# One 128-channel GpSimd add for a batch's logits instead of two 64-channel ones, and a new table of places

## The chip, the cores and the metric

The kernel runs on one core of a Trainium2 chip. The time is the device time of one execution in microseconds (us), and less is better. Engines are named as the profile names them: PE (TensorE matmuls; PEld its weight loads), DVE (VectorE), ACT (ScalarE), POOL (GpSimd), SP (the queue that issues most DMAs).

## The reference, cut to what matters

Two layers stand behind one another. The first is attention with a hash mask, for 4 batches of 8 heads, 768 positions and 64 columns a head; the second is a soft mixture of 8 experts with 4 slots each, over the 3,072 rows of 512 columns that the first one gives.

```python
mask = q_bucket[:, :, :, None] == k_bucket[:, :, None, :]      # 6 sign bits of q @ proj, k @ proj
scores = np.where(mask, scale * q @ k.T, -1e9)
attn = softmax(scores); x = (attn @ v) as (batch*position, head*column)
logits = x @ phi                                  # 3072 x 32
d = softmax of logits over the 3072 rows;  slot_input = d.T @ x
slot_out[e] = relu(slot_input[e] @ w1[e]) @ w2[e] # 8 experts
out = softmax of logits over the 32 slots @ slot_out
```

## The kernel before, in words

The 32 heads run through one software pipeline. Of a head, `smax` (L692) multiplies the keys with the queries once for the row maxima, and `most` (L701, L704) takes these on DVE out of two PSUM buffers, so PE can be at most two such products ahead of DVE. `shift` and `shift_rows` (L730 to L744) turn the maxima into a row of the operand: DVE, one PE transpose, an ACT copy, and a DMA on the SP queue (L744, told under the helper's line L600, as `XY<-mr`). `scores` (L755) multiplies a second time with the shift included, `exps` (L761) takes the exponential on ACT, `av` (L782) multiplies with v, and `acc` (L769, L772) adds the exponentials' tiles on POOL for the denominator, one 128x768 add at a time.

Heads go in pairs. Ahead of each pair `split_hi` (L592, ACT) and `split_lo` (L596) cut q and k in two parts; `split_lo` is one 128x768 subtraction on DVE and one on POOL, both with two operands in SBUF. After a pair, `pair_sum`, `pair_turn`, `pair_rec`, `pair_log`, `pair_add` and `pair_x` (L789 to L843) normalise it, write x and add its share of the logits to a tile `lacc` (128x384). The two halves of `lacc`'s 128 channels hold two partial sums, of even and odd heads.

After four pairs a batch is complete. `batch_both` (L885) adds the two halves and puts the sum on both: ACT copies channels 64 to 127 of `lacc` to channels 0 to 63 of `dl` (L889), then POOL adds twice on 64 channels (L891), first into the upper half of `dl`, then in place into the lower one. `batch_max` (L902 to L910) takes the maxima on DVE, and `batch_exp`, `batch_turn`, `batch_slots` and the like carry the batch into the slots. That happens inside the pipeline for batches 0 to 2; the last batch is done at the end by `one_sum` to `one_fold`, without `batch_both`.

The order of the work is written by hand and no tool moves it: three tables, `WHEN` (a place for each step of a pair), `FIRST` and `LAST` (for the first and the last heads), give each step a place counted in slots of a sixth of a head; `at` (L1043) puts the steps in a list, the list is sorted by place, and the steps are issued in that order. Each engine and the SP queue then run their own instructions strictly in this order. Weights of the experts are loaded between the heads (`load_weights`, 512 KB a piece). After the last head come the expert multiplications (L1198, L1251) and the output (L1274).

Of the kernel before, what the change touches and what calls it, by code (L numbers as in the profile page):

```python
# [76 lines left out]

FIRST = {('bits', 0): -102.0988,
 ('first_x', 0): -24.247,
 ('first_x', 1): -39.392,  # L80
 ('first_x', 2): -29.078,
 ('first_x', 3): -19.8151,
 ('load', 4, 0): -5.2093,
 ('load', 4, 1): -3.4609,
 ('bits', 2): -21.6367,
 ('split_hi', 2): -5.8363,
 ('split_lo', 2, 0): 0.2624,
 ('split_lo', 2, 1): -4.3782,
 ('spread_y', 2): -4.8648,
 ('spread_bits', 2): -12.8087,  # L90
 ('spread_l', 2): 6.144,
 ('spread_x', 2): 3.6219,
 ('smax', 1, 0, 0): -22.4884,
 ('smax', 1, 0, 1): -14.425,
 ('smax', 1, 1, 0): -13.675,
 ('smax', 1, 1, 1): -18.5454,
 ('smax', 1, 2, 0): -15.9696,
 ('smax', 1, 2, 1): -10.3836,
 ('smax', 1, 3, 0): -10.2744,
 ('smax', 1, 3, 1): -13.2403,  # L100
 ('smax', 1, 4, 0): -12.705,
 ('smax', 1, 4, 1): -11.4718,
 ('smax', 1, 5, 0): -8.4134,
 ('smax', 1, 5, 1): -17.6068,
 ('first_y', 1): -98.0409,
 ('first_y', 2): -23.6654,
 ('spread_y', 1): -34.1549,
 ('spread_l', 0): -19.5111,
 ('spread_bits', 1): -31.1275,
 ('bits_rest',): -39.0243,  # L110
 ('bits_copy', 0): -61.5875,
 ('bits_copy', 1): -49.0932,
 ('first_w', 0, 0): -52.9271,
 ('first_w', 0, 1): -45.0627,
 ('copy_ident',): -30.4055,
 ('bits_out',): -17.6073,
 ('shift_first', 0): -28.1207,
 ('rows_first', 0): -22.8276,
 ('shift_first', 1): -21.3284,
 ('rows_first', 1): -19.3923,  # L120
 ('most', 1, 0): -21.0299,
 ('most', 1, 2): -12.6994,
 ('most', 1, 3): -17.9276,
 ('most', 1, 4): -14.489,
 ('most', 1, 6): -5.6202,
 ('most', 1, 7): -10.9525,
 ('most', 1, 8): -7.0455,
 ('most', 1, 10): -4.4109,
 ('most', 1, 11): -16.3298,
 ('bits_first', 1): -52.2068,  # L130
 ('split_hi', 0): -104.3439,
 ('split_lo', 0, 0): -33.2942,
 ('split_lo', 0, 1): -24.2451,
 ('spread_x', 0): -18.4484,
 ('load_v', 0): -49.1631,
 ('smax', 0, 0, 0): -57.7206,
 ('scores', 0, 0, 0): -18.4489,
 ('most', 0, 0): -31.1109,
 ('exps', 0, 0): -16.2704,
 ('smax', 0, 0, 1): -54.4021,  # L140
 ('scores', 0, 0, 1): -17.5476,
 ('smax', 0, 1, 0): -48.1338,
 ('scores', 0, 1, 0): -16.9955,
 ('most', 0, 2): -29.8189,
 ('exps', 0, 2): -12.7003,
 ('smax', 0, 1, 1): -89.3202,
 ('scores', 0, 1, 1): -7.715,
 ('most', 0, 3): -45.7527,
 ('exps', 0, 3): -4.37,
 ('smax', 0, 2, 0): -81.0645,  # L150
 ('scores', 0, 2, 0): -13.5826,
 ('most', 0, 4): -32.0633,
 ('exps', 0, 4): -8.1301,
 ('smax', 0, 2, 1): -44.5826,
 ('scores', 0, 2, 1): -9.075,
 ('smax', 0, 3, 0): -38.6124,
 ('scores', 0, 3, 0): -5.9648,
 ('most', 0, 6): -29.6441,
 ('exps', 0, 6): -4.235,
 ('smax', 0, 3, 1): -38.4796,  # L160
 ('scores', 0, 3, 1): -14.8362,
 ('most', 0, 7): -28.5666,
 ('exps', 0, 7): -9.8986,
 ('smax', 0, 4, 0): -28.5933,
 ('scores', 0, 4, 0): -17.6084,
 ('most', 0, 8): -28.1478,
 ('exps', 0, 8): -12.8511,
 ('smax', 0, 4, 1): -25.4573,
 ('scores', 0, 4, 1): -13.1315,
 ('smax', 0, 5, 0): -23.7083,  # L170
 ('scores', 0, 5, 0): -1.5997,
 ('most', 0, 10): -22.8582,
 ('exps', 0, 10): 2.4486,
 ('smax', 0, 5, 1): -26.4348,
 ('scores', 0, 5, 1): -2.4708,
 ('most', 0, 11): -24.7664,
 ('exps', 0, 11): 2.5416,
 ('av', 0, 0): -11.6598,
 ('acc', 0, 1): 2.9017,
 ('av', 0, 1): -1.251,  # L180
 ('acc', 0, 2): 3.8826,
 ('av', 0, 2): -0.8419,
 ('acc', 0, 3): 4.5951,
 ('av', 0, 3): -0.6937,
 ('acc', 0, 4): 4.8395,
 ('av', 0, 4): 4.2016,
 ('acc', 0, 5): 11.46,
 ('av', 0, 5): 9.6883,
 ('spread_l', 1): -28.2578,
 ('spread_x', 1): -17.2822,  # L190
 ('load_v', 1): -33.0257,
 ('scores', 1, 0, 0): 1.3496,
 ('exps', 1, 0): 3.8687,
 ('scores', 1, 0, 1): 4.6498,
 ('scores', 1, 1, 0): 7.2362,
 ('exps', 1, 2): 8.0704,
 ('scores', 1, 1, 1): 4.1294,
 ('exps', 1, 3): 5.5945,
 ('scores', 1, 2, 0): 0.8493,
 ('exps', 1, 4): 3.2616,  # L200
 ('scores', 1, 2, 1): 1.752,
 ('scores', 1, 3, 0): 3.2247,
 ('exps', 1, 6): 5.1221,
 ('scores', 1, 3, 1): 10.8661,
 ('exps', 1, 7): 12.8423,
 ('scores', 1, 4, 0): 2.9321,
 ('exps', 1, 8): 10.0997,
 ('scores', 1, 4, 1): 6.0124,
 ('scores', 1, 5, 0): 9.855,
 ('exps', 1, 10): 11.8275,  # L210
 ('scores', 1, 5, 1): 10.5008,
 ('exps', 1, 11): 13.3899,
 ('shift', 1): -3.8039,
 ('shift_rows', 1): -2.6775,
 ('av', 1, 0): 11.9568,
 ('acc', 1, 1): 8.8476,
 ('av', 1, 1): 12.6368,
 ('acc', 1, 2): 11.415,
 ('av', 1, 2): 12.6451,
 ('acc', 1, 3): 14.0042,  # L220
 ('av', 1, 3): 12.9619,
 ('acc', 1, 4): 18.9427,
 ('av', 1, 4): 13.579,
 ('acc', 1, 5): 21.4429,
 ('av', 1, 5): 16.4939,
 ('load', 2, 0): -49.4921,
 ('load', 2, 1): -52.2068,
 ('load_v', 2): 10.2435,
 ('smax', 2, 0, 0): -4.103,
 ('scores', 2, 0, 0): 16.667,  # L230
 ('most', 2, 0): -2.8532,
 ('exps', 2, 0): 16.9649,
 ('smax', 2, 0, 1): 5.9825,
 ('scores', 2, 0, 1): 13.8757,
 ('smax', 2, 1, 0): 6.6523,
 ('scores', 2, 1, 0): 15.6577,
 ('most', 2, 2): 8.8854,
 ('exps', 2, 2): 16.8927,
 ('smax', 2, 1, 1): -0.3316,
 ('scores', 2, 1, 1): 13.8393,  # L240
 ('most', 2, 3): 2.2782,
 ('exps', 2, 3): 14.9992,
 ('smax', 2, 2, 0): 2.8055,
 ('scores', 2, 2, 0): 13.5895,
 ('most', 2, 4): 6.6529,
 ('exps', 2, 4): 16.0579,
 ('smax', 2, 2, 1): -1.9582,
 ('scores', 2, 2, 1): 17.72,
 ('smax', 2, 3, 0): 1.2515,
 ('scores', 2, 3, 0): 19.3082,  # L250
 ('most', 2, 6): 3.5218,
 ('exps', 2, 6): 19.3709,
 ('smax', 2, 3, 1): -3.7661,
 ('scores', 2, 3, 1): 16.8244,
 ('most', 2, 7): 0.5334,
 ('exps', 2, 7): 17.2995,
 ('smax', 2, 4, 0): 4.0474,
 ('scores', 2, 4, 0): 17.7324,
 ('most', 2, 8): 8.0087,
 ('exps', 2, 8): 19.7556,  # L260
 ('smax', 2, 4, 1): 5.8646,
 ('scores', 2, 4, 1): 19.2004,
 ('smax', 2, 5, 0): 8.5568,
 ('scores', 2, 5, 0): 20.167,
 ('most', 2, 10): 9.3556,
 ('exps', 2, 10): 20.2925,
 ('smax', 2, 5, 1): 4.1508,
 ('scores', 2, 5, 1): 17.3078,
 ('most', 2, 11): 8.6656,
# [1073 lines left out]
```

## Time and profile before

| | |
|---|---|
| median of 3 runs | 485.52 us (481.4, 485.52, 1116.75) |
| profiled execution | 484.55 us, its span 482.8 us |
| mean granted TensorE clock | 0.972 |
| PE busy | 452.3 us (94%), 3975 matmuls |
| DVE busy | 361.5 us (75%) |
| ACT busy | 276.9 us (57%) |
| POOL busy | 356.2 us (74%) |
| chain that ended last | PE 85%, DVE 6%, DMA 4%, ACT 2% |

The span is the time from the first to the last instruction of the profiled execution. A share of busy time is a mean over the whole span; the chain is the sequence of instructions and waits that ended last, followed back from the end.

### The profile page before, as it was taken

To read this page: it belongs to the slowest core of one execution; us is meant where nothing else is said; L and a number is where in the kernel's file an instruction comes from. 1 tells how busy PE (TensorE), PEld (TensorE's weight loads), DVE (VectorE), ACT (ScalarE), POOL (GpSimd) and SP (SyncE) were. 2 spreads that over 40 slices of the span, in tenths; PEclk is the share of its full clock that TensorE was granted. 3 is DMA by queue.
4 is the path that set the end of the run, shared out by engine and by line. 5 is a ranking of instruction groups with operands and counts; after the bars stand their busy time and mean duration, and the time that the engine had idled before them with its cause. 6 is when DMAs were issued, how large, how long until landed. Compare 5 with 4: busy or idle time off the path is not lost.

```text
span 482.8 us, 10644 instructions
## 1 busy us (share of the span) xinstructions
PE 452.3 (94%) x3975; PEld 280.5 (58%) x3975; DVE 361.5 (75%) x669; ACT 276.9 (57%) x568; POOL 356.2 (74%) x223
## 2 busy tenths in 40 slices
...
GB/s 190 123 190 159 136 150 152 164 160 210 153 92 205 135 216 150 226 139 228 136 142 143 202 157 169 201 170 176 98 183 128 67 167 331 342 380 331 412 302 304
DMA packets 37703, 93.18 MB, mean 193 GB/s; under 512 B 7106, under 2 KB 13380, under 8 KB 37652
## 3 DMA queue, kind: packets, MB, share of 16 engines
...
q8 instruction: 31, 0.51, 0.4%
q10 hardware_dynamic: 240, 0.34, 0.2%
...
## 4 chain that ended last, share of the span: by engine, by line
PE 85%; DVE 6%; DMA 4%; ACT 2%; issue 1%; SPq 0%; DVEq 0%; ACTq 0%
PE st L755 28%; PE av L782 23%; PE smx L692 15%; DVE w L596 4%; PE qs L1251 3%; PE qh L1198 3%; PE mi L639 3%; PE mi L794 2%; PE mi L819 2%; DMA w<-w 1%; PE mi L740 1%; PE av L548 1%; DMA XY<-mr 1%; PE mi L957 1%; ACT w L592 1%
## 5 line engine op out<-in xcount | busy, mean ns | idle before, releaser
L772 POOL TENSOR_TENSOR acc<-acc,pt 128x768 f32<-128x768 f32 x125 | 232.7, 1865 | 11.9 <-ACT pt L761 6.7
L761 ACT ACTIVATE pt<-st 128x512 f32<-128x512 f32 x288 | 163.5, 594 | 89.0 <-PE st L755 87.2
L755 PE MATMUL st<-XY 128*128 128x256 f32 (+1 forms) x768 | 181.4, 348 | 2.1 <-DMA XY<-mr 1.2
L704 DVE TENSOR_REDUCE mx<-smx 128x1 f32<-128x512 f32 x192 | 131.6, 688 | 49.0 <-PE smx L692 46.3
L755 PEld LDWEIGHTS st<-XY 128*128 128x128 f32 x768 | 127.7, 194 | 23.6 <-issue 4.5
L692 PE MATMUL smx<-XY 96*128 96x256 f32 (+1 forms) x384 | 123.2, 362 | 15.6 <-DVE mx L704 14.8
L782 PE MATMUL av<-pt,v 128*32 128x384 f32 x1536 | 137.7, 489 | 0.0
L692 PEld LDWEIGHTS smx<-XY 96*128 96x128 f32 x384 | 71.4, 194 | 49.0 <-DVE mx L704 18.8
L782 PEld LDWEIGHTS av<-pt,v 128*32 128x32 f32 x1536 | 45.4, 109 | 67.7 <-issue 55.0
L769 POOL TENSOR_TENSOR acc<-pt 128x768 f32<-128x768 f32 x32 | 58.6, 1832 | 32.9 <-ACT pt L761 32.9
L701 DVE TENSOR_REDUCE mx<-smx 128x2 f32<-128x512 f32 x96 | 65.6, 685 | 4.7 <-PE smx L692 3.8
L596 DVE TENSOR_TENSOR w<-raw,w 128x768 fp32r<-128x768 f32 x14 | 37.5, 2677 | 1.9 <-issue 0.5
L596 POOL TENSOR_TENSOR w<-raw,w 128x768 fp32r<-128x768 f32 x16 | 35.1, 2196 | 0.0
L797 ACT ACTIVATE sm<-mi,eps 128x384 f32<-128x384 f32 x15 | 8.7, 579 | 30.4 <-PE mi L794 30.4
L592 ACT CAST w<-raw 128x768 fp32r<-128x768 f32 x30 | 23.6, 831 | 0.5 <-DMA XY<-w 0.2
L609 ACT CAST XY<-w 64x768 fp32r<-64x768 f32 x30 | 23.3, 825 | 0.0
L786 ACT COPY avs<-av 128x384 f32<-128x384 f32 x32 | 15.2, 476 | 12.2 <-PE av L782 12.0
L842 DVE TENSOR_TENSOR xq<-mi,r 128x384 f32<-128x384 f32 x30 | 16.7, 558 | 2.2
L841 DVE STREAM_TRANSPOSE mi<-avs 128x384 f32<-128x384 f32 x30 | 17.4, 582 | 0.8 <-ACT mr L743 0.7
L811 ACT COPY r<-rt 64x12 f32<-64x12 f32 x60 | 11.9, 199 | 7.1 <-DVE rt L803 6.4
L1251 PE MATMUL qs<-w 128*32 128x128 f32 (+1 forms) x360 | 14.9, 304 | 0.0
L801 DVE STREAM_TRANSPOSE sm<-sm 128x384 f32<-128x384 f32 x15 | 8.7, 578 | 7.4 <-ACT sm L797 7.2
...
## 6 DMA issues: line engine op xcount, KB each, us to landing
...
```

The costliest lines, as they stand in the source:

```text
L592: nc.scalar.copy(st[h]["w4"][:, 2 * x], st[h]["raw", x])
L596: (nc.vector if h > 2 and x == 0 else nc.gpsimd).tensor_tensor(out=w[:, 2 * x + 1], in0=st[h]["raw", x], in1=w[:, 2 * x], op=ALU.subtract)
L609: nc.scalar.copy(s["Y"][0:64, x], s["w4"][0:64, 2 * x])
L692: nc.tensor.matmul(pt[:, o:o + b - a], s["Y"][0:96, 0, t * P:(t + 1) * P], s["Y"][0:96, 1, a:b], start=True, stop=True)
L701: nc.vector.tensor_reduce(out=mx[:, n - 1:n + 1], in_=s["sm_ps", n - 1].rearrange("p (a x) -> p a x", a=2), axis=AX.X, op=ALU.max)
L704: nc.vector.reduce_max(out=mx[:, n:n + 1], in_=s["sm_ps", n], axis=AX.X)
L755: nc.tensor.matmul(pt[:, o:o + b - a], x[:, 1, i * P:(i + 1) * P], x[:, 0, a:b], start=first, stop=not first)
L761: nc.scalar.activation(s["P", n // 4][:, 512 * u:512 * u + 512], s["st_ps", n - (n % 4 == 2)], AF.Exp, scale=D ** -0.5)
L769: nc.gpsimd.tensor_tensor(out=s["acc"], in0=pr[:, 0:S], in1=pr[:, S:2 * S], op=ALU.add)
L772: eng.tensor_tensor(out=s["acc"], in0=s["acc"], in1=pr[:, a * S:(a + 1) * S], op=ALU.add)
L782: nc.tensor.matmul(s["av"][2 * e + 32 * c:2 * e + 32 * c + 32, 0:HC], s["v"][:, i, e:e + 32], pr[:, o + c * HC:o + (c + 1) * HC], start=(i ...
L1251: nc.tensor.matmul(pos[i][32 * j:32 * j + 32, 0:w], hTs[g][:, f, 32 * j:32 * j + 32], wt[1, x, 2 * g + f // 4, j][:, (f % 4) * HM + o:(f % ...
```

## The change

In `batch_both` ACT now makes two copies of 64 channels, each half of `lacc` to the other half of `dl`, and POOL adds `lacc` to `dl` on all 128 channels in one instruction, in place. And all numbers in `WHEN`, `FIRST` and `LAST` are new; the steps and their keys are the same. Most numbers move by less than one slot. The tables are cut here to the entries near the batch's end and those that are moved past a queue's other work.

```diff
-        nc.scalar.copy(dl[0:64], lacc[64:128])
-        for x in (1, 0):
-            nc.gpsimd.tensor_tensor(out=dl[64 * x:64 * x + 64], in0=lacc[0:64], in1=dl[0:64], op=ALU.add)
+        for x in range(2):
+            nc.scalar.copy(dl[64 * x:64 * x + 64], lacc[64 - 64 * x:128 - 64 * x])
+        nc.gpsimd.tensor_tensor(out=dl, in0=lacc, in1=dl, op=ALU.add)
...
- 'split_lo': [-9.8385, -9.8378],
+ 'split_lo': [-8.8537, -10.0635],
- 'shift_rows': [-2.1527, 0.4391],
+ 'shift_rows': [-2.0369, 1.2347],
- 'pair_x': [25.7118, 30.2518],
+ 'pair_x': [26.9559, 31.3802],
- 'batch_both': 24.1116,
- 'batch_max': 26.5961,
- 'batch_exp': 31.1234,
+ 'batch_both': 23.3631,
+ 'batch_max': 27.5587,
+ 'batch_exp': 32.2161,
- 'batch_scale': 58.0306,
+ 'batch_scale': 38.5308,
- 'load_weights': 29.1076,
+ 'load_weights': 33.735,
...
```

## Rows read from the trace of the kernel before

**Rows 1.** Stretches, one pair each: us, each engine's busy time (instructions), clock, DMA.
```profile
125.79:158.11 32.32, 27.43 (x246) 17.23 (x250) 28.34 (x50) 16.75 (x35) 22.18 (x14) 0.89 0.50 137
158.11:181.63 23.52, 23.52 (x198) 14.87 (x202) 18.48 (x36) 16.31 (x35) 22.56 (x16) 1.00 0.66 185
...
228.77:260.92 32.15, 27.20 (x246) 16.93 (x250) 28.35 (x49) 16.94 (x36) 22.09 (x14) 0.89 0.51 138
...
284.49:309.46 24.97, 23.75 (x199) 14.90 (x202) 19.76 (x36) 15.60 (x31) 23.03 (x15) 1.00 0.64 178
...
333.02:365.83 32.81, 27.86 (x246) 17.64 (x250) 28.46 (x49) 16.96 (x36) 22.14 (x14) 0.90 0.50 136
```

**Rows 2.** PE's waits: who waited for whom, us in total, times, longest.
```profile
PE smx L692 <- DVE mx L704: 14.8, 3, 5.0
```

**Rows 3.** Stretches behind these waits, columns as in the first group.
```profile
141.90:148.70 6.80, 4.48 (x13) 3.71 (x14) 4.83 (x15) 1.79 (x3) 3.79 (x2) 0.50 0.73 241
244.30:251.10 6.80, 3.84 (x10) 3.17 (x11) 5.23 (x14) 1.22 (x3) 4.29 (x3) 0.50 0.64 208
350.10:356.90 6.80, 5.39 (x17) 4.60 (x18) 4.88 (x13) 1.79 (x3) 2.82 (x2) 0.50 0.74 251
```

**Rows 4.** The chain that ended last: start, us, what.
```profile
135.62 6.60 DVE w L596
...
238.59 6.61 DVE w L596
...
342.85 6.60 DVE w L596
```

**Rows 5.** DVE in order of time, behind the first of them: start, us, instruction.
```profile
142.15 0.54 DVE L902 TENSOR_REDUCE ml<-dl 64x1 f32<-64x384 f32 x1
...
143.48 0.68 DVE L704 TENSOR_REDUCE mx<-smx 128x1 f32<-128x512 f32 x1
```

**Rows 6.** POOL in order of time at the first batch's end.
```profile
132.17 2.10 POOL L891 TENSOR_TENSOR dl<-lacc,dl 64x384 f32<-64x384 f32 x2
...
134.23 1.83 POOL L772 TENSOR_TENSOR acc<-acc,pt 128x768 f32<-128x768 f32 x1
...
136.02 1.83 POOL L772 TENSOR_TENSOR acc<-acc,pt 128x768 f32<-128x768 f32 x1
137.80 1.85 POOL L596 TENSOR_TENSOR w<-raw,w 128x768 fp32r<-128x768 f32 x1
...
139.60 1.80 POOL L772 TENSOR_TENSOR acc<-acc,pt 128x768 f32<-128x768 f32 x1
...
141.48 2.40 POOL L772 TENSOR_TENSOR acc<-acc,pt 128x768 f32<-128x768 f32 x1
```

**Rows 7.** All DVE instructions of L596: count, ns shortest/median/longest, first and last start.
```profile
L596 DVE TENSOR_TENSOR w<-raw,w x14: 972/1784/6612, 41.1 to 375.6; 128x768 fp32r<-128x768 f32 x14
```

**Rows 8.** POOL and DVE in order of time, in a pair without a batch's end.
```profile
87.45 1.83 POOL L772 TENSOR_TENSOR acc<-acc,pt 128x768 f32<-128x768 f32 x1 [0.75 <-ACT pt L761]
89.25 2.55 POOL L596 TENSOR_TENSOR w<-raw,w 128x768 fp32r<-128x768 f32 x1
...
88.32 1.78 DVE L596 TENSOR_TENSOR w<-raw,w 128x768 fp32r<-128x768 f32 x1
```

**Rows 9.** Groups by line: count, busy us in all, mean ns of one, idle before.
```profile
L891 POOL TENSOR_TENSOR dl<-lacc,dl 64x384 f32<-64x384 f32 x6 | 6.1, 1009 | 0.5
...
L1002 POOL TENSOR_TENSOR lacc<-lacc,cs 128x192 f32<-128x192 f32 x3 | 1.5, 509 | 2.7 <-DVE cs L1001 2.7
...
L889 ACT COPY dl<-lacc 64x384 f32<-64x384 f32 x3 | 1.5, 493 | 0.0
```

**Rows 10.** The chain that ended last, in two later places: start, us, what.
```profile
62.92 4.01 PE av L782 x48
...
301.18 4.62 DMA XY<-mr
```

**Rows 11.** PE in order of time, with the idle time before it.
```profile
305.94 0.94 PE L755 MATMUL st<-XY 128*128 128x256 f32 x4 [1.22 <-DMA XY<-mr]
```

**Rows 12.** The last stretch, columns as in the first group.
```profile
452.00:482.80 30.80, 22.75 (x434) 17.20 (x426) 9.58 (x17) 9.11 (x19) 0.00 (x0) 0.95 0.83 325
```

More of the change, by code (lines that the diff above doesn't have):

```diff
@@ L78 @@
[L78 to L269, printed above, removed]
- ('exps', 2, 11): 17.7319,
- ('shift', 2): 10.3201,
- ('shift_rows', 2): 11.4595,
- ('spread_y', 3): -0.608,
- ('spread_bits', 3): -0.3442,
- ('spread_l', 3): 2.2492,
- ('spread_x', 3): 6.2796}
@@ new lines @@
+WHEN = {'load': -16.9234,
+ 'bits': -14.3717,
+ 'bits_over': -14.2655,
+ 'split_hi': -11.2327,
+ 'split_lo': [-8.8537, -10.0635],
+ 'spread': [[-10.9434, -8.8759, -5.5323, -4.0719], [-9.1735, -8.8228, -9.2009, -8.7942]],
+ 'load_v': [-2.0194, 0.6857],
+ 'smax': [[-5.575, -5.3023, -4.4327, -3.0295, -4.0086, -3.6335, -3.5262, -3.6649, -2.6064, -2.4574, -2.4398, -2.9107], [-7.944, -7.6273, -7.2504, -7.1653, -6.0491, -1.7544, -1.1252, -6.235, -2.2797, -0.308, -0.306, -0.5541]],
+ 'scores': [[5.5336, 6.5595, 7.2456, 5.3311, 4.8322, 7.6515, 7.8464, 5.8622, 8.3628, 7.2153, 7.2449, 6.0119], [2.9829, 3.2589, 3.3422, 2.8511, 5.6361, 2.9563, 3.2566, 3.4627, 4.4862, 5.1968, 5.5762, 4.7924]],
+ 'shift': [-2.3114, 0.6368],
+ 'shift_rows': [-2.0369, 1.2347],
+ 'acc': [[8.3761, 8.826, 9.5057, 10.2774, 11.0382], [5.0375, 6.238, 7.6971, 8.2168, 8.677]],
+ 'av': [[8.2731, 8.3246, 9.7304, 9.8775, 9.8827, 9.9536], [6.3913, 6.4111, 8.4627, 8.834, 8.8375, 9.6647]],
+ 'pair_sum': 21.6006,
+ 'pair_turn': 21.816,
+ 'pair_rec': 22.3657,
+ 'pair_log': 21.8834,
+ 'pair_x': [26.9559, 31.3802],
+ 'pair_add': 22.6172,
+ 'batch_both': 23.3631,
+ 'batch_max': 27.5587,
+ 'batch_exp': 32.2161,
+ 'batch_turn': 32.4089,
+ 'batch_scale': 38.5308,
+ 'batch_slots': 33.428,
+ 'batch_weigh': 33.4073,
+ 'batch_share': 33.5326,
+ 'batch_arrange': 33.6799,
+ 'load_weights': 33.735,
+ 'most': [[-5.349, -4.1424, -2.8414, -3.7102, -3.3152, -3.3833, -2.3128, -2.33, -2.6082], [-6.0949, -4.6558, -4.0, -3.3235, -0.4133, -3.3242, -1.3496, 0.6306, -0.0306]],
+ 'exps': [[6.8485, 7.9413, 5.9426, 5.2012, 8.5439, 6.9083, 9.1384, 8.8492, 7.1258], [3.3029, 3.7302, 3.1641, 6.1125, 3.8755, 3.858, 4.9531, 6.2821, 6.0829]]}
@@ new lines @@
+FIRST = {('bits', 0): -101.543,
+ ('first_x', 0): -31.129,
+ ('first_x', 1): -41.8778,
+ ('first_x', 2): -30.4433,
+ ('first_x', 3): -30.3229,
+ ('load', 4, 0): -20.6184,
+ ('load', 4, 1): -22.0264,
+ ('bits', 2): -22.3793,
+ ('split_hi', 2): -6.4967,
+ ('split_lo', 2, 0): -6.2049,
+ ('split_lo', 2, 1): 4.2464,
+ ('spread_y', 2): -5.5328,
+ ('spread_bits', 2): -9.495,
+ ('spread_l', 2): 0.4844,
+ ('spread_x', 2): 10.106,
+ ('smax', 1, 0, 0): -22.1248,
+ ('smax', 1, 0, 1): -13.2036,
+ ('smax', 1, 1, 0): -12.9101,
+ ('smax', 1, 1, 1): -18.1026,
+ ('smax', 1, 2, 0): -17.8604,
+ ('smax', 1, 2, 1): -9.3553,
+ ('smax', 1, 3, 0): -7.5577,
+ ('smax', 1, 3, 1): -12.9317,
+ ('smax', 1, 4, 0): -11.3896,
+ ('smax', 1, 4, 1): -9.8965,
+ ('smax', 1, 5, 0): -9.5129,
+ ('smax', 1, 5, 1): -17.8875,
+ ('first_y', 1): -70.4282,
+ ('first_y', 2): -25.835,
+ ('spread_y', 1): -32.8086,
+ ('spread_l', 0): -26.4249,
+ ('spread_bits', 1): -32.0262,
+ ('bits_rest',): -43.2032,
+ ('bits_copy', 0): -84.8785,
+ ('bits_copy', 1): -62.3488,
+ ('first_w', 0, 0): -59.6648,
+ ('first_w', 0, 1): -48.3736,
+ ('copy_ident',): -31.9762,
+ ('bits_out',): -21.3411,
+ ('shift_first', 0): -26.5007,
+ ('rows_first', 0): -24.5304,
+ ('shift_first', 1): -24.1286,
+ ('rows_first', 1): -20.1473,
+ ('most', 1, 0): -18.4307,
+ ('most', 1, 2): -7.4183,
+ ('most', 1, 3): -16.9542,
+ ('most', 1, 4): -9.787,
+ ('most', 1, 6): -5.1583,
+ ('most', 1, 7): -9.5635,
+ ('most', 1, 8): -6.2791,
+ ('most', 1, 10): -5.5547,
+ ('most', 1, 11): -12.2143,
+ ('bits_first', 1): -45.885,
+ ('split_hi', 0): -102.9618,
+ ('split_lo', 0, 0): -41.287,
+ ('split_lo', 0, 1): -36.1424,
+ ('spread_x', 0): -17.4895,
+ ('load_v', 0): -42.7266,
+ ('smax', 0, 0, 0): -66.2181,
+ ('scores', 0, 0, 0): -18.7815,
+ ('most', 0, 0): -50.4976,
+ ('exps', 0, 0): -17.2045,
+ ('smax', 0, 0, 1): -62.6355,
+ ('scores', 0, 0, 1): -17.9918,
+ ('smax', 0, 1, 0): -51.3723,
+ ('scores', 0, 1, 0): -17.8711,
+ ('most', 0, 2): -48.2669,
+ ('exps', 0, 2): -12.9238,
+ ('smax', 0, 1, 1): -98.8458,
+ ('scores', 0, 1, 1): -10.1891,
+ ('most', 0, 3): -52.6139,
+ ('exps', 0, 3): -4.8827,
+ ('smax', 0, 2, 0): -85.0962,
+ ('scores', 0, 2, 0): -16.1452,
+ ('most', 0, 4): -52.3583,
+ ('exps', 0, 4): -10.592,
+ ('smax', 0, 2, 1): -40.7031,
+ ('scores', 0, 2, 1): -6.4783,
+ ('smax', 0, 3, 0): -40.2028,
+ ('scores', 0, 3, 0): -6.2462,
+ ('most', 0, 6): -31.6036,
+ ('exps', 0, 6): -1.9218,
+ ('smax', 0, 3, 1): -38.6758,
+ ('scores', 0, 3, 1): -17.0204,
+ ('most', 0, 7): -28.1042,
+ ('exps', 0, 7): -11.3811,
+ ('smax', 0, 4, 0): -34.0318,
+ ('scores', 0, 4, 0): -19.9306,
+ ('most', 0, 8): -25.7979,
+ ('exps', 0, 8): -17.3079,
+ ('smax', 0, 4, 1): -32.1625,
+ ('scores', 0, 4, 1): -3.3204,
+ ('smax', 0, 5, 0): -28.2818,
+ ('scores', 0, 5, 0): -2.445,
+ ('most', 0, 10): -24.3782,
+ ('exps', 0, 10): 4.1274,
+ ('smax', 0, 5, 1): -38.2463,
+ ('scores', 0, 5, 1): -7.0941,
+ ('most', 0, 11): -26.6457,
+ ('exps', 0, 11): -4.1733,
+ ('av', 0, 0): -12.1583,
+ ('acc', 0, 1): 0.7279,
+ ('av', 0, 1): -1.3879,
+ ('acc', 0, 2): 7.173,
+ ('av', 0, 2): -0.5655,
+ ('acc', 0, 3): 8.4793,
+ ('av', 0, 3): 0.0999,
+ ('acc', 0, 4): 9.835,
+ ('av', 0, 4): 5.7756,
+ ('acc', 0, 5): 17.1671,
+ ('av', 0, 5): 9.03,
+ ('spread_l', 1): -26.4126,
+ ('spread_x', 1): -22.0888,
+ ('load_v', 1): -43.5022,
+ ('scores', 1, 0, 0): 4.0342,
+ ('exps', 1, 0): 7.1746,
+ ('scores', 1, 0, 1): 6.1496,
+ ('scores', 1, 1, 0): 7.2149,
+ ('exps', 1, 2): 7.7127,
+ ('scores', 1, 1, 1): 4.9004,
+ ('exps', 1, 3): 7.8766,
+ ('scores', 1, 2, 0): 2.3532,
+ ('exps', 1, 4): 5.2847,
+ ('scores', 1, 2, 1): 4.2418,
+ ('scores', 1, 3, 0): 4.2753,
+ ('exps', 1, 6): 6.376,
+ ('scores', 1, 3, 1): 10.7846,
+ ('exps', 1, 7): 11.4272,
+ ('scores', 1, 4, 0): 5.9274,
+ ('exps', 1, 8): 7.2041,
+ ('scores', 1, 4, 1): 10.0553,
+ ('scores', 1, 5, 0): 10.4872,
+ ('exps', 1, 10): 11.2833,
+ ('scores', 1, 5, 1): 10.6839,
+ ('exps', 1, 11): 12.0139,
+ ('shift', 1): -3.9487,
+ ('shift_rows', 1): -2.8308,
+ ('av', 1, 0): 11.537,
+ ('acc', 1, 1): 8.6417,
+ ('av', 1, 1): 12.8701,
+ ('acc', 1, 2): 11.7694,
+ ('av', 1, 2): 13.8093,
+ ('acc', 1, 3): 13.9532,
+ ('av', 1, 3): 13.8116,
+ ('acc', 1, 4): 14.1314,
+ ('av', 1, 4): 15.1614,
+ ('acc', 1, 5): 20.1319,
+ ('av', 1, 5): 15.2142,
+ ('load', 2, 0): -32.877,
+ ('load', 2, 1): -60.9886,
+ ('load_v', 2): 11.0565,
+ ('smax', 2, 0, 0): -5.5302,
+ ('scores', 2, 0, 0): 17.6176,
+ ('most', 2, 0): -3.5974,
+ ('exps', 2, 0): 18.1194,
+ ('smax', 2, 0, 1): 8.1394,
+ ('scores', 2, 0, 1): 15.3467,
+ ('smax', 2, 1, 0): 8.2921,
+ ('scores', 2, 1, 0): 16.8081,
+ ('most', 2, 2): 9.3459,
+ ('exps', 2, 2): 17.2301,
+ ('smax', 2, 1, 1): 1.8058,
+ ('scores', 2, 1, 1): 17.1714,
+ ('most', 2, 3): 3.8596,
+ ('exps', 2, 3): 17.8602,
+ ('smax', 2, 2, 0): 5.2297,
+ ('scores', 2, 2, 0): 16.7503,
+ ('most', 2, 4): 7.7132,
+ ('exps', 2, 4): 16.8569,
+ ('smax', 2, 2, 1): 2.2573,
+ ('scores', 2, 2, 1): 18.586,
+ ('smax', 2, 3, 0): 3.7836,
+ ('scores', 2, 3, 0): 19.6113,
+ ('most', 2, 6): 4.0817,
+ ('exps', 2, 6): 20.4115,
+ ('smax', 2, 3, 1): -4.1755,
+ ('scores', 2, 3, 1): 18.7783,
+ ('most', 2, 7): -1.3343,
+ ('exps', 2, 7): 20.2235,
+ ('smax', 2, 4, 0): 4.8484,
+ ('scores', 2, 4, 0): 18.5681,
+ ('most', 2, 8): 5.0106,
+ ('exps', 2, 8): 19.6458,
+ ('smax', 2, 4, 1): 5.853,
+ ('scores', 2, 4, 1): 20.3643,
+ ('smax', 2, 5, 0): 6.3928,
+ ('scores', 2, 5, 0): 20.4695,
+ ('most', 2, 10): 8.9077,
+ ('exps', 2, 10): 20.6661,
+ ('smax', 2, 5, 1): 5.8631,
+ ('scores', 2, 5, 1): 18.3007,
+ ('most', 2, 11): 8.5725,
+ ('exps', 2, 11): 18.9253,
+ ('shift', 2): 9.6657,
+ ('shift_rows', 2): 11.4277,
+ ('spread_y', 3): -1.4584,
+ ('spread_bits', 3): 6.0557,
+ ('spread_l', 3): 5.9188,
+ ('spread_x', 3): 9.3718}
```

259 lines of the change are left out of this document (118 added, 141 removed).

## The prediction

> **What bounds the kernel now.** I read the list of busy times first (PE 94%), then cut the span at the same instruction of each pair, to see where PE isn't full. An ordinary pair takes 23.52 us, and PE is busy in all of them: no new order of steps can make it shorter. The three pairs that hold a batch's end take 32.32, 32.15 and 32.81 us, at a mean clock of 0.89 to 0.90 [rows 1]. So the question is what these three have that the others lack.
>
> The list of waits answers: PE waited three times for a row maximum of DVE, 14.8 us in all [rows 2]. The granted clock, cut finely, then shows a stretch of 6.80 us at 0.50 (the level of 1.2 GHz) at each of the three places, with PE busy for 4.48, 3.84 and 5.39 us [rows 3]. What kept DVE is in the chain: one `split_lo` subtraction of 6.60 us at each place [rows 4], where the median of all 14 is 1.78 and the shortest 0.97 [rows 7]. Behind it DVE runs `batch_max` and only then the maximum that PE wants, which begins at 143.48 [rows 5].
>
> Why 6.60 us? In an ordinary pair the subtraction begins (88.32) while POOL's add runs (87.45 to 89.28); it ends at 90.10, 0.82 us after that add, and POOL's next instruction takes 2.55 us where such a one takes 1.85 elsewhere [rows 6, 8]. So DVE gets in between two POOL instructions, though the second starts without a gap, and POOL pays about 0.7 us. At the batch's end it is passed over at 136.06, 137.85 and 139.65, and gets in only at 141.40, where for once POOL leaves a gap of 0.08 us (139.60 + 1.80 to 141.48); the others begin 0.04 us before their predecessor's end [rows 6]. What stands in front of these instructions and of no others is the pair of narrow adds of `batch_both`, on 64 channels, 2.10 us [rows 6].
>
> My reading: during the second narrow add the half of POOL that serves the other 64 channels has nothing to do and runs on, one microsecond ahead, into the next add. From there on some part of POOL is always reading until an instruction waits and the halves meet. DVE needs them all to pause.
>
> By the Trainium skill (SBUF — State Buffer, Who interferes with whom), a DVE instruction with two SBUF inputs and a GpSimd one that reads SBUF exclude one another, and the first to start holds the port for its whole instruction. By that rule alone the subtraction would have waited for one add, until 136.06, and then run: some 1.3 us, an estimate by that page; the trace has 6.60. A second place (GPSIMD Engine Reference, Instruction dispatch) says that each of GpSimd's cores serves 16 partitions and starts the next instruction as soon as its own share is done; with that the trace agrees.
>
> **The change, part by part.**
>
> *One POOL add on 128 channels.* Removed: 2.10 us of POOL in each of three batches [rows 6]. Added: one add of 128x384; the trace has no such row, but the time goes with the columns: 0.51 us for 128x192, 1.01 for 64x384, 1.83 for 128x768 [rows 6, 9]. I take 1.01, between 0.92 (half of 1.83) and 1.02 (twice 0.51). POOL gains 3 x 1.09 = 3.3 us; that is off the path, since PE never waits for POOL in this region.
>
> *No skew.* All channels now work in every POOL instruction of the pipeline, so the subtraction should get in at the first end of an add. I take the median, 1.78 us; bounds: 0.97 (shortest seen) and 1.83 + 0.82 = 2.65 (a whole add, then its own run). It ends 4.82 us earlier, and the maximum behind it with it: of a mean wait of 4.93 us 0.1 is left. At the upper bound 0.98 is left; at the lower nothing, and nothing more is gained. `batch_max` stays in front of that maximum in the new order, from 142.15 to 143.48 [rows 5], and is what would be late next. The sum: 14.8 us less 3 x 0.1 gives 14.5.
>
> *The clock.* With no wait of 5 us the clock should stay at 1.00: in the pair from 284.49, PE waited 1.22 us and the clock was 1.00 throughout [rows 1, 11]. PE was busy for 4.48 + 3.84 + 5.39 = 13.71 us at half clock [rows 3]; at full clock half, 6.9 us, goes. Bounds: 0 and 6.9; I take all of it. Check: the three batch pairs are 97.28 - 3 x 23.52 = 26.7 us over ordinary ones [rows 1]; less 14.8 and 6.9 leaves 5.0, 1.7 us a batch, for 48 matmuls more in each (x246 against x198).
>
> *A second ACT copy.* 3 x 0.49 us [rows 9]. ACT is busy 16.75 us of the 32.32 [rows 1], so it fits, and the exponentials queued behind it are 0.49 us later at most. POOL's add waits for it; the new order has head 8's last add ahead of it, as cover. If that is gone POOL stands 0.5 us, less than it saved.
>
> *All places anew.* Sorting both tables gives each queue's order. Of PE's 1,052 steps 604 keep their place and 928 move by at most two; DVE 435 of 455, ACT 389 of 441, POOL 193 of 197, SP 188 of 225. Near the batch's end `split_lo` on DVE keeps its place behind the same maxima and ahead of `batch_max` (only `pair_x` and one maximum change places), and POOL's own `split_lo` goes one add later. Further moves: on POOL, `batch_scale` of batches 1 and 2 (128x1) goes 14 and 17 steps forward, long after `batch_exp`, which feeds it; on SP, half of the weight loads move nine steps, directly ahead of the even head's row transfer, and the v load goes ahead of the two q/k loads. Between the even row's issue and its first use stand 19 PE steps (20 before), six of them `av`, 4.01 us alone [rows 10]; for odd heads 12, as before. I cost the moves at nothing: PE has no idle time in ordinary pairs to lose or win, and the cover is that work. Bounds: the first heads and the tail are rearranged most, and PE idles 8.05 of the last 30.80 us [rows 12]; 4 us either way.
>
> Sum: 14.5 + 6.9 = 21.4 us; I leave 0.3 for the second copy and the third batch. From the profiled execution's 484.55 (span 482.8 and 1.75 around it; 0.2% under the median of 485.52) this gives **463.5 us**, 0.955 of the median.
>
> **The rivals.**
>
> *Part of the wait stays.* In its new place the subtraction misses one more POOL instruction, or the maximum comes late for another reason: 1.83 us more in each batch, 463.5 + 5.5 = 469; if the clock falls too, 476. For it: DVE is busy 28.35 us of these 32, so it has little slack [rows 1]. Against it: 6.6 us of that are the wait itself.
>
> *The skew isn't it.* POOL is merely behind, and DVE is passed over as long as adds follow without a gap. Then the shorter add helps by its 1.09 us alone: 484.55 - 3 x 1.09 = 481.3; with this cause the change doesn't do what it says. Against it: in the ordinary pair DVE got in at a boundary without a gap [rows 8], and the median of all 14 subtractions is 1.78 us, though POOL is busy 92 to 96% of the two ordinary pairs shown (22.56 of 23.52, 23.03 of 24.97) [rows 1, 7]. The Trainium skill (SBUF — State Buffer, Who interferes with whom) comes near to this case: where only the order of starting counts, the width of an add changes nothing but its own length, and the time would be this rival's. The three passes at 136.06, 137.85 and 139.65 speak against it.
>
> *Slower: the rows land late.* The new SP order lets a head's shifted row land after PE wants it, in each of 15 pairs. One such row already took 4.62 us, and PE waited 1.22 [rows 10, 11]. Price: 15 x W on top of 463.5; it decides the sign from W = 2.1 us (495), and at W = 2.5 it gives 501. For it: 512 KB of weights now stand right ahead of the even head's row. Against it: the 4.01 us of `av` and 13 more steps that cover it, and the odd rows have three transfers ahead of them in both orders.
>
> **How the numbers follow.** All waits gone, 459 to 467: 0.75. Part stays, 467 to 477: 0.13. Not the skew, about 481: 0.08. Rows late, near 501: 0.03; what I haven't seen, 0.01. The range 457 to 477 holds the first two and the bounds of the moves. A measurement of this kernel tells about 2% from no change, so faster means under 475.8: the first case and most of the second, 0.87; the same 0.10, the rest of the second and the third; slower 0.03.
>
> **What would show it.** Right: `split_lo` on DVE at no more than 2.65 us in all 14 places; PE's wait for the row maxima under 3 us in all; clock 1.00 from the first heads to the tail; batch pairs near 25.2 us (23.52 + 1.7); one `batch_both` add of about 1.0 us. Wrong: a subtraction near 6 us behind the wide add (the skew isn't the cause), or ordinary pairs over 23.6 us with PE waiting for row transfers (the places cost).

## The result, and the profile after

The changed kernel takes 467.23 us (median of 4), the kernel before 484.69 us in the same comparison: a ratio of 0.967, 95% interval 0.9595 to 0.9746. One of the four runs of the kernel before took 1,116.75 us, and the ratio leaves it out. The forecast was 463.5 us, 0.955. The profiled execution took 470.04 us, its span 468.2.

First the pairs, cut as before (us, then each engine's busy time and instructions, clock, DMA); the second row is an ordinary pair, the others hold a batch's end. The last row is the tail behind the last such pair.

```profile
127.70:153.25 25.55, 25.55 (x247) 15.55 (x242) 22.65 (x51) 17.12 (x36) 21.95 (x13) 1.00 0.64 176
153.25:176.79 23.54, 23.54 (x198) 14.76 (x194) 19.03 (x36) 16.28 (x35) 22.51 (x17) 1.00 0.69 183
224.66:250.25 25.59, 25.57 (x247) 15.53 (x243) 22.60 (x49) 17.30 (x37) 21.68 (x13) 1.00 0.65 175
321.09:346.67 25.58, 25.57 (x247) 15.54 (x243) 22.60 (x49) 17.31 (x37) 21.92 (x13) 1.00 0.66 176
346.67:468.20 121.53, 107.75 (x1138) 60.98 (x1130) 65.49 (x133) 50.92 (x118) 51.48 (x39) 0.93 0.76 273
```

Against [rows 1] the three batch pairs went from 97.28 us in all to 76.72, PE is busy in all of them, and the clock is 1.00. The waits and the half clock of [rows 2, 3] are gone there. The same stretch of the tail in the kernel before:

```profile
365.76:482.80 117.04, 105.10 (x1143) 59.61 (x1142) 62.86 (x134) 50.89 (x118) 53.36 (x40) 0.97 0.80 281
```

So of 20.56 us won at the batches' ends the tail gives 4.49 back. The remaining 1.5 us lie ahead: the first two pairs took 2.3 us longer in this execution and the ordinary ones 0.8 less. Other executions with the same first places end that stretch between 34.56 and 35.45 us, against 34.59 before and 36.88 here, so the 2.3 us are mostly scatter.

POOL and DVE at the first batch's end, in order of time (start, us, instruction), answer to [rows 4, 6]:

```profile
134.81 1.01 POOL L891 TENSOR_TENSOR dl<-lacc,dl 128x384 f32<-128x384 f32 x1 [1.82 <-ACT dl L890]
...
135.98 1.84 POOL L772 TENSOR_TENSOR acc<-acc,pt 128x768 f32<-128x768 f32 x1 [0.16 <-ACT pt L761]
...
137.91 2.44 POOL L772 TENSOR_TENSOR acc<-acc,pt 128x768 f32<-128x768 f32 x1
...
137.24 1.41 DVE L596 TENSOR_TENSOR w<-raw,w 128x768 fp32r<-128x768 f32 x1
```

The wide add takes 1.01 us, as forecast. POOL stands 1.82 us ahead of it, waiting for the copies; PE never waits for POOL here, so that costs nothing. The subtraction asks at 137.24, gets in at 137.82 (135.98 + 1.84) and is through in 1.41 us. All 14 of them (count, ns shortest, median, longest) answer to [rows 7]:

```profile
L596 DVE TENSOR_TENSOR w<-raw,w x14: 948/950/1405, 43.7 to 356.5; 128x768 fp32r<-128x768 f32 x14
```

Even the ordinary ones went from 1.78 to 0.95. In the new order all of them but the first, which starts while POOL waits for ACT, start within the 0.08 us that POOL leaves between two adds to one accumulator, or up to 0.21 us ahead of it, and so have next to nothing to wait for:

```profile
88.31 1.84 POOL L772 TENSOR_TENSOR acc<-acc,pt 128x768 f32<-128x768 f32 x1 [2.37 <-ACT pt L761]
...
90.23 2.58 POOL L772 TENSOR_TENSOR acc<-acc,pt 128x768 f32<-128x768 f32 x1
...
90.17 0.95 DVE L596 TENSOR_TENSOR w<-raw,w 128x768 fp32r<-128x768 f32 x1
```

That wins nothing, since PE had no idle time there.

### The profile page after: what moved, and what is told of

The parts are those of the page before. It is cut to its first block, busy times and chain, and to the rows that moved or that the text cites. A ratio compares the mean times of both kernels' runs of the same rounds, so it can differ in the third digit from the quotient of the medians.

```text
span 468.2 us, 10643 instructions
## 1 busy us (share of the span) xinstructions
PE 452.0 (97%) x3975; PEld 277.8 (59%) x3975; DVE 341.7 (73%) x669; ACT 277.6 (59%) x571; POOL 352.7 (75%) x220
## 4 chain that ended last, share of the span: by engine, by line
PE 88%; DVE 6%; DMA 2%; SPq 1%; issue 1%; ACT 0%; DVEq 0%
PE st L755 27%; PE av L782 25%; PE smx L692 16%; PE qh L1198 3%; PE qs L1251 3%; PE mi L639 2%; PE mi L819 2%; PE mi L794 2%; PE mi L740 1%; PE av L548 1%; DMA XY<-mr 1%; PE mi L957 1%; PE qh L1274 1%; DMA raw<-qk 1%; SPq L600 1%
## 5 line engine op out<-in xcount | busy, mean ns | idle before, releaser
L772 POOL TENSOR_TENSOR acc<-acc,pt 128x768 f32<-128x768 f32 x125 | 238.2, 1908 | 21.8 <-ACT pt L761 16.4
L761 ACT ACTIVATE pt<-st 128x512 f32<-128x512 f32 x288 | 160.0, 596 | 59.1 <-PE st L755 53.8
L755 PE MATMUL st<-XY 128*128 128x512 f32 (+1 forms) x768 | 174.4, 342 | 0.3 <-DMA XY<-mr 0.3
L755 PEld LDWEIGHTS st<-XY 128*128 128x128 f32 x768 | 122.1, 190 | 20.2 <-ACT pt L761 3.3
L692 PE MATMUL smx<-XY 96*128 96x256 f32 (+1 forms) x384 | 120.9, 357 | 0.3
L692 PEld LDWEIGHTS smx<-XY 96*128 96x128 f32 x384 | 69.7, 190 | 33.7 <-DVE mx L704 14.2
L596 POOL TENSOR_TENSOR w<-raw,w 128x768 fp32r<-128x768 f32 x16 | 29.4, 1841 | 1.8 <-DMA XY<-bt 1.8
L596 DVE TENSOR_TENSOR w<-raw,w 128x768 fp32r<-128x768 f32 x14 | 14.7, 1052 | 1.0 <-ACT w L592 1.0
L1198 PE MATMUL qh<-w,siT 128*32 128x512 f32 x128 | 15.1, 628 | 0.0
L639 PE MATMUL mi<-raw,pb 128*32 128x384 f32 x120 | 14.1, 510 | 0.9 <-DMA raw<-qk 0.9
```

What stands on the lines that cost most here:

```text
L596: (nc.vector if h > 2 and x == 0 else nc.gpsimd).tensor_tensor(out=w[:, 2 * x + 1], in0=st[h]["raw", x], in1=w[:, 2 * x], op=ALU.subtract)
L692: nc.tensor.matmul(pt[:, o:o + b - a], s["Y"][0:96, 0, t * P:(t + 1) * P], s["Y"][0:96, 1, a:b], start=True, stop=True)
L755: nc.tensor.matmul(pt[:, o:o + b - a], x[:, 1, i * P:(i + 1) * P], x[:, 0, a:b], start=first, stop=not first)
L761: nc.scalar.activation(s["P", n // 4][:, 512 * u:512 * u + 512], s["st_ps", n - (n % 4 == 2)], AF.Exp, scale=D ** -0.5)
L772: eng.tensor_tensor(out=s["acc"], in0=s["acc"], in1=pr[:, a * S:(a + 1) * S], op=ALU.add)
L1198: nc.tensor.matmul(ph[fh][32 * j:32 * j + 32], siT[:, k, 4 * g + j, :], wt[0, g, k, j][:, fh * 512:(fh + 1) * 512], start=(k == 0), stop=( ...
```

## The experiments

Two theories stood at first. **Skew:** a narrow add lets one half of POOL run ahead, and the subtraction cannot get in until a POOL instruction waits for the one directly before it. **Backlog:** DVE is passed over as long as POOL's adds follow without a gap, whatever their width. A third, **places**, says that the new order did it. Each ratio below is to the kernel before, in runs on the same chip, with its 95% interval.

**The wide add alone**, with all places of before:

```diff
-        nc.scalar.copy(dl[0:64], lacc[64:128])
-        for x in (1, 0):
-            nc.gpsimd.tensor_tensor(out=dl[64 * x:64 * x + 64], in0=lacc[0:64], in1=dl[0:64], op=ALU.add)
+        for x in range(2):
+            nc.scalar.copy(dl[64 * x:64 * x + 64], lacc[64 - 64 * x:128 - 64 * x])
+        nc.gpsimd.tensor_tensor(out=dl, in0=lacc, in1=dl, op=ALU.add)
```

> The kernel before with the two copies and the one 128-channel add, all places as before. Theory (skew: a 64-channel add lets the idle half of POOL run ahead into the next instruction, and DVE's subtraction with two SBUF operands cannot get in until a POOL instruction waits for its direct predecessor): the three subtractions of 6.6 us fall to at most 2.65 us, PE's wait for row maxima to under 3 us in all, no half clock there; 461 to 466 us. Rival (backlog: DVE is passed over as long as POOL's adds follow without a gap, whatever their width): only POOL's 1.09 us per batch is won, 480 to 482. Rival (places: the new order took the wait away, not the add): 484.

Measured: 465.6 us, ratio 0.957 (0.950 to 0.964); in a second comparison 467.3, 0.9635 (0.9593 to 0.9676). The profiled run took 462.72. POOL and DVE at the first batch's end:

```profile
132.40 1.00 POOL L891 TENSOR_TENSOR dl<-lacc,dl 128x384 f32<-128x384 f32 x1 [0.54 <-ACT dl L890]
...
133.35 1.84 POOL L772 TENSOR_TENSOR acc<-acc,pt 128x768 f32<-128x768 f32 x1
...
135.15 1.84 POOL L772 TENSOR_TENSOR acc<-acc,pt 128x768 f32<-128x768 f32 x1
...
136.94 2.56 POOL L596 TENSOR_TENSOR w<-raw,w 128x768 fp32r<-128x768 f32 x1
...
135.73 2.07 DVE L596 TENSOR_TENSOR w<-raw,w 128x768 fp32r<-128x768 f32 x1 [0.44 <-issue]
```

The instructions behind the add are those of [rows 6], in the same order, each beginning before its predecessor ends. Yet the subtraction gets in at 136.99, the first boundary after it asks, and takes 2.07 us instead of 6.60. Backlog falls here, and so does places as the only cause: the add alone is enough.

**The new places alone**: the same edit the other way round, in the changed kernel:

```diff
-        for x in range(2):
-            nc.scalar.copy(dl[64 * x:64 * x + 64], lacc[64 - 64 * x:128 - 64 * x])
-        nc.gpsimd.tensor_tensor(out=dl, in0=lacc, in1=dl, op=ALU.add)
+        nc.scalar.copy(dl[0:64], lacc[64:128])
+        for x in (1, 0):
+            nc.gpsimd.tensor_tensor(out=dl[64 * x:64 * x + 64], in0=lacc[0:64], in1=dl[0:64], op=ALU.add)
```

> The changed kernel's places with the one copy and the two 64-channel adds of before. In this order the second POOL add behind the narrow ones waits for its direct predecessor (same accumulator), so POOL leaves a gap there. Skew theory as stated: the halves meet at that gap, the three subtractions take at most 3 us, and the time is that of the changed kernel plus at most 3 x 1.1 us: 467 to 471. Skew that lasts whatever follows: subtractions of 5 to 7 us, 484 to 490. Places theory: 467.

Measured: 467.92 us, 0.9612 (0.9553 to 0.967), as the changed kernel. The longest subtraction takes 1.83 us:

```profile
134.10 1.83 POOL L772 TENSOR_TENSOR acc<-acc,pt 128x768 f32<-128x768 f32 x1
...
136.01 2.44 POOL L772 TENSOR_TENSOR acc<-acc,pt 128x768 f32<-128x768 f32 x1
...
134.92 1.83 DVE L596 TENSOR_TENSOR w<-raw,w 128x768 fp32r<-128x768 f32 x1
```

In this order the second add behind the narrow ones adds to the same accumulator as the first and waits for it: POOL leaves 0.08 us (134.10 + 1.83 to 136.01), and DVE gets in there. So either half of the change takes the stall away alone, and the second half does it by this gap. I had seen the first only.

**A third narrow add**, so that both halves have the same work (places of before):

```diff
+        nc.gpsimd.tensor_tensor(out=dl[64:128], in0=dl[64:128],
+                                in1=ones[64:128, 0:1].broadcast_to([64, HC]), op=ALU.mult)
```

> The kernel before with one more POOL instruction in each batch: behind the second narrow add a third one, on the other 64 channels (dl times one, so it changes no value), so that both halves of POOL have the same work and end together. POOL has more instructions than before, no fewer. Skew theory: the third runs beside the second and costs POOL almost nothing; the three subtractions get in at the first boundary, at most 2.65 us each; 461 to 467 us. Backlog theory: POOL is no shorter, the subtractions stay at 6.6 us or grow by 1 us; 484 to 490.

Measured: 468.87 us, 0.9633 (0.9564 to 0.9702), over the 461 to 467 expected; in its profile PE waits 2.9 us for row transfers. The subtractions take at most 2.28 us, though POOL has more to do than before, and the one below gets in at an end without a gap (136.12 + 1.84 = 137.96). That speaks against backlog. It does not show that equal work is what helps:

```profile
134.14 1.00 POOL L891 TENSOR_TENSOR dl<-lacc,dl 64x384 f32<-64x384 f32 x1
...
135.22 0.82 POOL L892 TENSOR_TENSOR dl<-dl,ones 64x384 f32<-64x384 f32 x1
...
136.12 1.84 POOL L772 TENSOR_TENSOR acc<-acc,pt 128x768 f32<-128x768 f32 x1
...
137.92 2.55 POOL L772 TENSOR_TENSOR acc<-acc,pt 128x768 f32<-128x768 f32 x1
...
136.51 2.26 DVE L596 TENSOR_TENSOR w<-raw,w 128x768 fp32r<-128x768 f32 x1
```

I had expected the third instruction to run beside the second; it ran behind it, and POOL left 0.08 us on either side of it, which by the skew theory would let the halves meet whatever their work.

**The same extra add, narrow or wide.** On top of the wide `batch_both`, twelve odd heads get one more POOL add that nobody reads, just ahead of their second add; only its channels differ, W being 64 or 128. The lines that set up `plain` (constants) and `aside` (384 columns) are cut, and so is the wide `batch_both`, shown above:

```diff
...
+        if n == 2 and h % 2 and 3 <= h <= 25:
+            nc.gpsimd.tensor_tensor(out=aside[0:W], in0=plain[0:W], in1=plain[0:W], op=ALU.add)
...
```

> The kernel before's places with the wide add, and in twelve of the pairs one more POOL add of 384 columns on 64 channels (constants into a tile that nobody reads), just ahead of the second add of the pair's odd head, so ahead of the stretch in which DVE's subtraction asks to get in. Skew theory: behind a narrow add the subtraction cannot get in at a boundary without a gap, now in ordinary pairs too; subtractions of 4 to 7 us in most of the twelve, PE waits for row maxima again, 480 to 520 us. Backlog theory: the same as with the add on 128 channels, since POOL's time is the same.

> The same with the additional twelve adds on all 128 channels: the same 384 columns, the same 1.0 us of POOL each, 12 us in all. Skew theory: no half runs ahead, subtractions of at most 2.7 us, 463 to 470 us. Backlog theory: POOL is as late as with the 64-channel adds, so the time is that of the other kernel.

Measured: 489.53 us with 64 channels, 1.0121 (1.0071 to 1.0171); 463.10 us with 128, 0.9566 (0.9524 to 0.9608). POOL is busy 362.1 and 363.0 us. In the rows of these two kernels L598 is `split_lo`, L763 `exps`, L771 the extra add and L776 `acc`. The first batch's end with 64 channels (the profiled run took 494.54 us):

```profile
135.96 0.81 POOL L771 TENSOR_TENSOR aside<-phs 64x384 f32<-64x384 f32 x1
...
136.75 1.83 POOL L776 TENSOR_TENSOR acc<-acc,pt 128x768 f32<-128x768 f32 x1
138.54 1.84 POOL L598 TENSOR_TENSOR w<-raw,w 128x768 fp32r<-128x768 f32 x1
140.34 1.79 POOL L776 TENSOR_TENSOR acc<-acc,pt 128x768 f32<-128x768 f32 x1
...
142.21 2.40 POOL L776 TENSOR_TENSOR acc<-acc,pt 128x768 f32<-128x768 f32 x1
...
136.53 6.43 DVE L598 TENSOR_TENSOR w<-raw,w 128x768 fp32r<-128x768 f32 x1 [0.41 <-issue]
```

and with 128:

```profile
135.48 0.81 POOL L771 TENSOR_TENSOR aside<-phs 128x384 f32<-128x384 f32 x1
...
136.26 2.55 POOL L776 TENSOR_TENSOR acc<-acc,pt 128x768 f32<-128x768 f32 x1
...
136.04 1.07 DVE L598 TENSOR_TENSOR w<-raw,w 128x768 fp32r<-128x768 f32 x1 [0.41 <-issue]
```

The same instruction of the same 0.81 us, ahead of the same queue: narrow, it brings the 6.60 us of [rows 4] back; wide, it costs nothing. This settles the width as the cause. My expectation missed in one point: I wanted 4 to 7 us in most of the twelve places, and only 4 stall, the three batches' ends and one ordinary pair (5.53 us). The rows of all twelve tell them apart. At two places (169.51 and 276.57) the subtraction asks before the extra add begins (at 169.37 and 276.28) and gets in ahead of it. At six, the add behind the narrow one starts 0.08 to 0.11 us after the end of ACT's last exponential, about the 0.08 us that POOL leaves behind a predecessor that it waits for: by these times it had only just become ready, and no half had work to run ahead to. At the four that stall, ACT was done 0.24 to 1.03 us before that start. One of the six, then the ordinary pair that stalls:

```profile
86.63 0.82 POOL L771 TENSOR_TENSOR aside<-phs 64x384 f32<-64x384 f32 x1
87.42 1.85 POOL L776 TENSOR_TENSOR acc<-acc,pt 128x768 f32<-128x768 f32 x1
...
86.26 1.08 ACT L763 ACTIVATE pt<-st 128x512 f32<-128x512 f32 x2 [1.39 <-PE st L757]
...
88.29 1.79 DVE L598 TENSOR_TENSOR w<-raw,w 128x768 fp32r<-128x768 f32 x1
...
298.43 0.82 POOL L771 TENSOR_TENSOR aside<-phs 64x384 f32<-64x384 f32 x1
299.22 1.83 POOL L776 TENSOR_TENSOR acc<-acc,pt 128x768 f32<-128x768 f32 x1
...
297.89 1.08 ACT L763 ACTIVATE pt<-st 128x512 f32<-128x512 f32 x2 [1.39 <-PE st L757]
...
299.93 5.53 DVE L598 TENSOR_TENSOR w<-raw,w 128x768 fp32r<-128x768 f32 x1
```

**The tail.** The wait that PE has in the tail of the changed kernel, and the half clock behind it:

```profile
PE smx L875 <- DVE avs L865: 3.2, 1, 3.2
```

```profile
409.80:423.50 13.70, 12.37 (x90) 7.70 (x94) 7.47 (x26) 4.75 (x13) 0.00 (x0) 0.50 0.59 210
```

The tail of the kernel before has half clock for 3.4 us, and 0.5 us of this wait. What is late is a DVE instruction of twelve columns, `one_r`'s addition (L858), which the two heads of the last pair run once each. Before:

```profile
L858 DVE TENSOR_SCALAR rt<-sm x1: 173/173/173, 424.3 to 424.3; 128x12 f32<-128x12 f32 x1
L858 DVE TENSOR_SCALAR rt<-dl x1: 173/173/173, 425.8 to 425.8; 128x12 f32<-128x12 f32 x1
```

After, with POOL beside it:

```profile
398.87 1.61 DVE L858 TENSOR_SCALAR rt<-sm 128x12 f32<-128x12 f32 x1
...
398.62 1.83 POOL L772 TENSOR_TENSOR acc<-acc,pt 128x768 f32<-128x768 f32 x1
...
407.21 1.74 DVE L858 TENSOR_SCALAR rt<-dl 128x12 f32<-128x12 f32 x1
...
407.94 0.98 POOL L1161 MEMSET siT<- 128x1024 f32 x1
```

Both end within 0.03 us of a POOL instruction's end: 400.48 against 400.45, 408.95 against 408.92. The new `LAST` puts the first under the last head's add, and the second under the fetch of `fold` (407.18 to 407.94) and the clearing of `siT`. To test it, POOL's last two go elsewhere, both at once, so that the clearing alone holds DVE out rests on the times above:

```diff
-            nc.gpsimd.dma_start(out=fold, in_=cst[:, C_FD:C_ALL])
+            nc.sync.dma_start(out=fold, in_=cst[:, C_FD:C_ALL])
-            nc.gpsimd.memset(siT, 0.0)
+            nc.scalar.mul(siT.rearrange("p k e s -> p (k e s)"), wt[0, 0, 0, 0], 0.0)
```

> The changed kernel with POOL's last two instructions taken off POOL: the fold matrix is fetched by the SP queue, and the zeros of siT are written by ACT. In the changed kernel a 128x12 DVE instruction of one_r (L858) that took 0.17 us before takes 1.74 us there, and ends when POOL's memset ends. Theory (port: this instruction too is kept out while POOL works): it falls to 0.2 us, PE's wait of 3.2 us behind it to about 1.6, and the half-clock stretch of 13.7 us gets shorter; 462 to 466. Rival (the tail waits for weights anyway): 466 to 468, as the changed kernel.

Measured: 463.09 us, 0.9527 (0.9442 to 0.9611). The second addition takes 0.17 us, the first still 1.62; PE's wait falls to 1.7 us and the half clock to 3.4. Then the first goes too, back to its old place:

```diff
- ('one_r', -2): -2.3986,
- ('one_rec', -2): -2.3733,
- ('one_mul', -2): 0.6174,
+ ('one_r', -2): 1.4545,
+ ('one_rec', -2): 3.1261,
+ ('one_mul', -2): 4.0867,
```

> The changed kernel with the quiet tail, and with one_r, one_rec and one_mul of head 30 at the places that they had before, behind the last head's adds. The first of the two 128x12 DVE instructions (L858) took 1.62 us in the quiet tail too, under POOL's add of the last head; theory (port): it falls to 0.2 us as well, and the tail is that of the kernel before; 460 to 463 us. Rival (the tail waits for something else): 463, as with the quiet tail.

> The changed kernel, once more, beside the two: 466 to 468 us, 3 to 5 us over the mended tail if the tail's two held instructions and the half clock behind them are what it lost against the forecast.

> The wide add with the places of before, once more, for a comparison on one chip with the two beside it: 461 to 466 us. If the new places are worth their tail, it is slower than the mended tail by about 2 us (26.25 against 25.55 us for a pair with a batch's end, three times); if they are not, the two are the same.

Measured on one chip: mended tail 462.44 us, 0.9545 (0.9513 to 0.9578); the changed kernel 468.12, 0.9663 (0.963 to 0.9695); the wide add with the old places 467.3, 0.9635 (0.9593 to 0.9676). Both additions take 0.174 us now, the tail 114.70 us instead of 122.87 in that comparison's profile of the changed kernel, and there is no half clock ahead of the last stretch:

```profile
L858 DVE TENSOR_SCALAR rt<-sm x1: 174/174/174, 400.7 to 400.7; 128x12 f32<-128x12 f32 x1
L858 DVE TENSOR_SCALAR rt<-dl x1: 174/174/174, 403.6 to 403.6; 128x12 f32<-128x12 f32 x1
```

This version beats both kernels, the changed one by 5.7 us where 3 to 5 were expected. Against the quiet tail it shows no gain in time (0.9545 and 0.9527 of the kernel before), so that the first addition cost PE anything is not shown; the 3.4 us of half clock that went with it are no more than tails in the old order differ by (none and 3.4 us in the wide add's two profiles, 6.8 with the third narrow add).

The wide add with the old places was expected at 461 to 466 us, 2 behind the mended tail; it came to 467.3, 4.9 behind. Its profile is 5.3 us the longer: 2.2 us in the three batch pairs, as expected, 1.6 in the tail and 1.5 in the first heads and the ordinary pairs, where row transfers landed late (PE waited 1.2 us for them). Its two comparisons differ by 1.7 us. Beside it, at 468.12 us, the changed kernel is no faster: what the new places gain at the batches' ends they lose in the tail.

## Why the prediction was right, and where it was not

*What bounded the batch's end.* Right: one subtraction, held out by POOL, then PE's wait, then half clock. All three vanish together, in the changed kernel and with the add alone.

*Skew as the cause.* Right. That the width does it is shown by the pair of extra adds. That one half of POOL runs ahead is inferred, since no trace shows the halves apart: the stall comes only where the next add could start early, and it ends at the first gap. The Trainium skill (GPSIMD Engine Reference, Instruction dispatch) says that a core of GpSimd starts on the next instruction when its own share is done; the stall by 64 channels alone agrees. What the prediction did not see is that the new places end the skew one add later by themselves, because the order puts two adds to one accumulator behind one another. So the changed kernel's own time speaks for no cause: it would have come without the wide add. The gap of 0.08 us at which DVE got in stood in [rows 6]; that the new order moves such a gap forward could have been read from the sorted tables.

*The sum.* PE's wait: 14.5 us forecast, 14.8 gone. Half clock: 6.9 forecast, all of it gone. The batch pairs came to 25.57 us, not 25.2, which is 1.1 us in all: the 48 additional matmuls and what stands around them cost about 2.0 us a batch and not 1.7. With the old places and the wide add they cost 2.7 (26.21 to 26.31 us a pair), so the new places gain 0.7 a batch there, which the forecast did not count.

*A second ACT copy.* Mis-sized, off the path: POOL was to stand 0.5 us for it at most, and stands 1.82, 2.07 and 1.82 us in the three batches, because ACT has other work ahead of the copies. That is more than the 1.09 us that the wide add saves, and PE feels neither.

*All places anew, costed at nothing.* This is the step that failed. Its bound was 4 us; the tail came out 4.2 to 5.8 us longer in the three profiles with these places (121.24, 121.53 and 122.87 against 117.04). I looked at PE's idle time and at each queue's length, and not at who stands on POOL while DVE runs a short instruction. `one_r` moved under POOL's work at two places, 1.4 and 1.6 us late each, and the half clock behind it was 13.70 us long, with PE busy for 12.37; at full clock that is 6.2 us less. In the profiled execution the sum closes: 21.1 us forecast, 14.6 won; of the 6.5 missing, 4.5 are in the tail, 0.5 in the batch pairs and 1.5 in the rest. With the tail mended the time is 462.4.

*The rivals.* Part of the wait stays: no, the subtractions are at 1.41 at most. Yet 467.23 lies in this rival's 467 to 477 and just outside the 459 to 467 of the case that came about: by the time alone, the wrong case would have been taken for the right one. Not the skew: refuted by the add alone. Rows late: PE waits 0.3 us in all for row transfers in this profile, 1.4 in the later one of the same kernel.
